# Two forward products of the second token block, in halves of 256 tokens, moved ahead of the first block's last two backward products

## The chip, the cores and the metric

The kernel runs on one core of a Trainium2 chip. The metric is the time of one execution in device microseconds; smaller is better. The core has five instruction streams that matter here, each of which runs its own list in order: TensorE (PE; its weight loads are shown as PEld), VectorE (DVE), ScalarE (ACT), GpSimd (POOL) and SyncE (SP), which here issues loads only. They meet through semaphores.

## The reference, cut to what matters

One call computes the output and all gradients of a mixture of two branches, for x of 2048 tokens by 1024 channels and a hidden width F of 3584:

```
g   = sigmoid((x * gate_w).sum(-1))          # one gate per token
a   = irfft2(rfft2(x) * (w_r + 1j * w_i))    # spectral branch
h   = x @ w1 + b1
out = g * a + (1 - g) * (relu(h) ** 2 @ w2 + b2)
```

and, for a given grad_out, the gradients of x, w_r, w_i, w1, b1, w2, b2 and gate_w. For the dense branch the backward pass needs db = (1 - g) * grad_out, then dh = 2 * relu(h) * (db @ w2.T), from which the gradients of w1, b1, w2 and x follow.

## The kernel before, in words

The kernel is one long program for TensorE with the other engines around it. It has an opening (up to about 80 us), in which x and grad_out are loaded, turned and first used; then the rest of the dense layer's forward and backward products, with the spectral branch's transforms dealt in between; then the gradients of w1 and w2, the gradient of x, and the output. Only the opening is touched by the change.

The tokens go in four blocks of 512 (`s` = 0 to 3), the hidden width in chunks of 128 rows; `fp` counts pairs of chunks and `c` the chunk in a pair. In the opening the first two pairs, so four chunks, go through all four blocks.

Per block of four tiles of 128 tokens, these steps follow one another:

- x is loaded by SyncE (`rows_of_x`, L1815), turned on TensorE into xT (`turn_x`, `turn_tile`, L709, through two PSUM buffers `pt`) and copied out of PSUM, mostly by ScalarE (L710).
- VectorE sums x * gate_w over the channels of each tile (`gate_of`, L724). `gate` (L727) makes 1 - g of the four sums on ScalarE (omg, L731, and gcol, L732) and multiplies the four tiles of grad_out by it on VectorE (L734).
- These four tiles (dbn) are turned on TensorE (`turn_grad`, L709) and copied to dbT, mostly by VectorE (L710).
- A forward product `forth(fp, s, c)` is eight matmuls of 128 x 512 (L820) into one PSUM bank (ph) and a ReLU on ScalarE (L821); after two of them ScalarE squares the pair (L795).
- A backward product `back_(fp, s, c)` is eight matmuls with w2T (L827) into a bank (pd), and one VectorE instruction (L831) that makes dh of it. Forward and backward products share two banks.

w2T is a part of w2 turned by the DMA while it is loaded. For these four chunks it is loaded in two halves, and the second half is read by the backward products of the second pair alone.

The first two forward products of the first block are already made in two parts of 256 tokens each: `half_hidden(c, h)` (L802) makes part `h` of chunk `c` with eight matmuls of 128 x 256 (L807). The first parts are issued as soon as two tiles of x are turned, and `hidden` (L813) adds the second part when the product's turn comes.

The order of all this is written out by hand: `mlp_in` is a generator that is advanced once per product, and the loop at L1865 takes a step of it between the turning of tiles, gates and loads. In the first round of that loop (`k` = 0) the steps are: three forward products; the turning of the first gradient tiles; the fourth forward product; the first backward product; x tiles 4 and 5 turned; the second backward product; x tiles 6 and 7 turned; the seventh step; stores, the gates of the second block, more loads of x, and the start of the spectral branch's first stage (`first_stage`, L743); the eighth step. The gradient tiles of the second block are turned in the next round.

`first_stage` adds and subtracts the halves of rows of x (`folds`, L270: L272, L273, L277, L278, L283 and L284 on VectorE, three small copies on ScalarE, L279 to L285), multiplies the result on TensorE (`row_stage`, L293; `column_stage`, L325). It reads x from tiles of its own (src), loaded by `ahead_to` (L736) on SyncE, two row tiles for one fold.

Within this order a scheduler of the framework places the instructions of each engine. `after(ins, earlier, NoSync)` (L250) ties an instruction in order behind another one without a semaphore; with the default it also waits. The first two instructions of a fold (L272 and L273), the gate sums L724 of all but the first block, and L293 are tied in this way to `later["last"]`, which is the newest L831 at the time when the line of the program is run. The third fold's loads (L741) wait for it.

Of the kernel before, what the change touches and what calls it, by code (L numbers as in the profile page):

```python
# [10 lines left out]
P = 128  # L11
# [130 lines left out]
def kernel(  # L142
# [107 lines left out]
    def after(ins, earlier, wait=mybir.DependencyClass.Sync):  # L250

        if earlier is not None:
            info = mybir.DependencyInfo(wait, mybir.DependencyReason.DATA)
            tc.add_manual_dep(ins.ins, earlier.ins.name, info, reason="paced")
# [440 lines left out]
    xT = xT_p.tile([P, DC, S], BF16, name="xT", tag="xT")  # L695
    dbT = xT_p.tile([P, DC, S], BF16, name="dbT", tag="dbT")

    later = {}
# [71 lines left out]
    def mlp_in():  # L770
# [5 lines left out]
        SW = 512  # L776
# [11 lines left out]
        def h_bank():  # L788
            return mps.tile([P, SW], FP32, name="ph", tag="ph", bufs=2)
# [9 lines left out]

        begun = {}  # L800

        def half_hidden(c, h):  # L802
            if h == 0:
                begun[c] = h_bank()
            part = slice(h * SW // 2, (h + 1) * SW // 2)
            for dc in range(DC):
                one = mm(  # L807
                    begun[c][:, part], lhsT=w1[0][:, dc, c * P : (c + 1) * P], rhs=xT[:, dc, part],
                    start=h + dc == 0, stop=dc == DC - 1, skip_group_check=True,
                )  # L810
            later.setdefault("halves", []).append(one)

        def hidden(fc, ss, w1g, rT):  # L813
            if fc in begun:
                half_hidden(fc, 1)
                ph = begun.pop(fc)
            else:
                ph = h_bank()
                for dc in range(DC):
                    later["newest"] = mm(ph[:], lhsT=w1g[:, dc, fc % 2 * P : (fc % 2 + 1) * P], rhs=xT[:, dc, ss], start=(dc == 0), stop=(dc == DC - 1))  # L820
            nc.scalar.activation(rT, ph[:], ACT.Relu, bias=b1col[:, fc : fc + 1])  # L821
# [14 lines left out]
        def load_w2(fg, earlier=None, halves=(0, FGW // 2)):  # L836

            if fg not in w2T:
                w2T[fg] = wb.tile([P, DC, FGW], BF16, name="w2T", tag="w2T", bufs=2)
            for h in halves:  # L840
                f0 = fg * FGW + h
                after(turned(w2T[fg][:, :, h : h + FGW // 2], B_w2[f0 : f0 + FGW // 2, :]), earlier)

        w1, h2, dh, rTs = {}, {}, {}, {}
# [3 lines left out]
        def load_w1(fp):  # L848
            w1[fp] = f1.tile([P, DC, PW], BF16, name="w1f", tag="w1f") if fp == 2 else wb.tile([P, DC, PW], BF16, name="w1g", tag="w1g", bufs=2)
            ld(out=w1[fp][:], in_=w1v[:, :, fp * PW : (fp + 1) * PW])  # L850
# [12 lines left out]
        def forth(fp, s, c, by_rows=False):  # L863
            first, at = (s % 2 == 0, s % 2) if by_rows else (c == 0, c)
            if first:
                pair[0] = new_rT()
            rT = pair[0][:, at, :]
            hidden(2 * fp + c, rows_(s), w1[fp], rT)
            rTs[fp, s, c] = rT
            if not first:  # L870
                out = h2_of(fp, s // 2)
                squared(pair[0][:], out[:, c] if by_rows else out[:, :, s % 2, :])
            if c == 1 and s % 2 == 1:
                store(h2T_scr, h2.pop((fp, s // 2)), fp, s // 2)
# [131 lines left out]
        load_w1(1)  # L1006
        yield
        half_hidden(0, 0), half_hidden(1, 0)
        load_w2(0, halves=(0,))
        yield  # L1010
        load_w2(0, halves=(FGW // 2,))
        yield
        waiting = []
        for s in range(4):
            for what in (forth, back_):
                for fp in range(2):
                    for c in range(2):
                        if s == 3 and what is back_:
                            waiting.append((fp, s, c))
                        else:  # L1020
                            what(fp, s, c)
                        if s == 2 and what is forth and fp + c == 0:
                            load_w2(1, later["last"])
                        yield
            if s == 1:
                load_w1(2)
        for _ in w_sums(2, True):
            pass
# [22 lines left out]
        for n, u in enumerate(units_):  # L1051
# [60 lines left out]
            waiting = [(u.fp, 2 * u.sp + j, c) for c, j in ((0, 0), (0, 1), (1, 1), (1, 0))]  # L1112
# [728 lines left out]
    warm(7)  # L1841

    units = mlp_in()
    rows_of_x(0, 2)
    vrow = f1.tile([FC + DC, P], BF16, name="vrow", tag="vrow")
# [143 lines left out]
```

## Time and profile before

| | |
|---|---|
| median of 3 runs | 1193.3 us (1192.56 to 1193.49) |
| the profiled execution's own time | 1191.93 us |
| its span, first to last instruction | 1190.2 us |
| TensorE busy | 1177.4 us, 7275 matmuls |
| VectorE / ScalarE / GpSimd busy | 895.3 / 531.5 / 387.6 us |
| DMA | 249.84 MB, mean 210 GB/s |

Lines of the profile give the start in us, the duration, the engine, the line of the program, the operation, what is written and read, and the count of like instructions in a row; in brackets stands the idle time of the engine just before, and what ended it. In the groups by line the columns are the busy time, the mean duration in ns, and the idle time before, with what ended most of it. Times are counted from the span's start.

### The profile page before, as it was taken

How to read it: one execution, taken by the hardware profiler on the slowest of the kernel's cores; microseconds unless marked ns; L12 is line 12 of the kernel's file. 1: busy time of each engine (PE TensorE's matmuls, PEld its weight loads, DVE VectorE, ACT ScalarE, POOL GpSimd, SP SyncE). 2: the span in 40 equal slices, each digit the busy share in tenths (PEclk: the TensorE clock that was granted, in tenths of full speed). 3: DMA queues.
4: the chain of work that ended last, by engine and by line, in shares of the span. 5: the costliest groups of instructions: out<-in, count | busy, mean ns of one | idle time of the engine just before them, and what ended most of it. 6: DMA issues, size and time to landing. Idle time of an engine off the chain costs nothing.

```text
span 1190.2 us, 19485 instructions
## 1 busy us (share of the span) xinstructions
PE 1177.4 (99%) x7275; PEld 640.5 (54%) x7275; DVE 895.3 (75%) x1598; ACT 531.5 (45%) x961; POOL 387.6 (33%) x618
## 2 busy tenths in 40 slices
PE   8999999999999999999999999999999999999998
PEld 5555555444444444444447999998544444444444
DVE  6888887788989887877637666676785777976757
ACT  5678888577777772444324666564100010000000
POOL 0234433555858573755231233221001110000000
PEclk9999999999999999999999999999999999999999
DMA  9997585677969779888997999995799999564530
GB/s 251 298 291 235 166 215 170 199 211 179 249 169 232 239 241 186 195 192 212 225 200 157 232 229 260 234 217 153 251 193 228 263 287 282 170 199 147 181 125 36
DMA packets 329464, 249.84 MB, mean 210 GB/s; under 512 B 187912, under 2 KB 287658, under 8 KB 328858
## 3 DMA queue, kind: packets, MB, share of 16 engines
q1 hardware_dynamic: 268352, 112.12, 44.2%
q0 software_dynamic: 35136, 111.72, 29.9%
q10 hardware_dynamic: 25882, 24.76, 7.0%
q8 instruction: 57, 0.93, 0.3%
q14 instruction: 37, 0.30, 0.1%
HBM read 114.82 MB, written 89.67 MB: 172 GB/s over the span
## 4 chain that ended last, share of the span: by engine, by line
PE 78%; DVE 14%; ACT 3%; issue 2%; DMA 2%; SPq 1%; ACTq 0%; DVEq 0%
PE pX L1275 15%; PE xX L1576 14%; PE pV L1275 12%; PE pd L827 11%; PE xV L1576 7%; PE ph L928 6%; PE xZ L1576 4%; PE ph L820 2%; PE pui L325 1%; DVE dhT L831 1%; DVE rT L947 1%; PE pki L635 1%; DVE tt L453 1%; PE pu L325 1%; PE pZ L928 1%
## 5 line engine op out<-in xcount | busy, mean ns | idle before, releaser
L827 PE MATMUL pd<-dbT,w2T 128*128 128x512 bf16 x896 | 210.1, 379 | 3.4 <-DMA w2T<-in_B_w_dram 1.5
L827 PEld LDWEIGHTS <-w2T 128*128 128x128 bf16 x896 | 86.4, 98 | 107.6 <-issue 6.2
L1576 PEld LDWEIGHTS <-dS 128*128 128x128 f16 x686 | 66.4, 98 | 79.0 <-issue 3.4
L831 DVE SCALAR_TENSOR_TENSOR dhT<-pd,rT 128x512 bf16<-128x512 f32 x112 | 76.6, 684 | 33.7 <-PE pd L827 32.9
L1627 POOL DMA_DIRECT2D out_dram<-ot x32 | 17.4, 544 | 246.1 <-DVE ot L1683 128.0
L1693 ACT ACTIVATE w2br<-w2br,dsc 128x512 f32<-128x512 bf16 x8 | 5.8, 724 | 174.5 <-DVE ot L1683 117.4
L1576 PE MATMUL xX<-oT,dS 128*128 128x512 f16 x336 | 76.4, 379 | 0.6 <-DVE eR L1605 0.5
L1291 ACT COPY u<-pX 128x512 f32<-128x512 f32 x56 | 32.8, 586 | 90.5 <-PE pX L1275 84.9
L1576 PEld LDWEIGHTS <-odd 128*128 128x128 bf16 (+1 forms) x462 | 44.8, 98 | 51.5 <-issue 0.9
L1576 PEld LDWEIGHTS <-even 128*128 128x128 bf16 (+1 forms) x448 | 43.6, 98 | 52.6 <-issue 0.7
L1275 PEld LDWEIGHTS <-T 128*128 128x128 f16 x672 | 64.6, 98 | 7.5 <-issue 0.2
L948 ACT ACTIVATE rT<-rT 128x512 bf16<-128x512 bf16 x69 | 43.4, 629 | 42.3 <-DVE rT L947 41.8
L795 ACT ACTIVATE h2T<-rT 128x1024 bf16<-128x1024 bf16 x56 | 59.6, 1065 | 0.2
L1295 DVE TENSOR_TENSOR whi<-pV,u 128x512 bf16<-128x512 f32 x28 | 19.3, 689 | 47.1 <-ACT u L1291 47.0
L491 POOL DMA_DIRECT2D y_scr<-pc x64 | 47.2, 738 | 22.7 <-DVE pc L488 12.9
L1275 PEld LDWEIGHTS <-S 128*128 128x128 f16 x336 | 32.5, 98 | 40.8 <-DVE S L1207 1.9
L453 DVE TENSOR_TENSOR tt<-x,w 128x1028 f16<-128x1028 f16 (+1 forms) x64 | 41.9, 689 | 11.0 <-issue 5.8
L1275 PEld LDWEIGHTS <-resL 128*128 128x128 bf16 x448 | 43.1, 98 | 4.9
L1275 PEld LDWEIGHTS <-resR 128*128 128x128 f16 (+1 forms) x448 | 42.9, 98 | 4.9 <-issue 0.2
L1295 DVE TENSOR_TENSOR wlo<-pV,u 128x512 bf16<-128x512 f32 x28 | 19.2, 687 | 32.0 <-PE pV L1275 31.9
L859 POOL DMA_DIRECT2D h2T_scr<-h2T x28 | 20.9, 746 | 67.1 <-ACT f L285 30.2
L239 POOL DMA_DIRECT2D r<-y_scr x48 | 28.0, 588 | 42.4 <-ACT re L614 33.1
(382 smaller groups left out, 2803.7 us busy)
## 6 DMA issues: line engine op xcount, KB each, us to landing
h2T_scr<-h2T POOLq DMA_DIRECT2D x28, 512.0 KB, 4.2
dhT_scr<-dhT POOLq DMA_DIRECT2D x28, 512.0 KB, 5.2
y_scr<-pc POOLq DMA_DIRECT2D x64, 128.0 KB, 4.2
ax_scr<-yo POOLq DMA_DIRECT2D x16, 512.0 KB, 5.3
out_dram<-ot POOLq DMA_DIRECT2D x31, 256.0 KB, 3.3
z<-z_scr ACTq DMA_DIRECT2D x60, 128.0 KB, 3.4
out_dram<-whi POOLq DMA_DIRECT2D x28, 256.0 KB, 5.2
out_dram<-wlo POOLq DMA_DIRECT2D x28, 256.0 KB, 4.8
```

The source lines that it names most:

```text
L239: st(out=a, in_=b) if stored else st(out=b, in_=a)
L453: V(out=tt[:, k, :, :, 0:W], in0=x[:, a : a + 2, :, 0:W], in1=by, op=ALU.mult)
L491: st(out=columns_of(y_scr, c, h), in_=pc[:, n])
L795: after(nc.scalar.activation(h2T, rT, ACT.Square), behind_, mybir.DependencyClass.NoSync)
L827: turn["PE"] = mm(pd[:], lhsT=w_[:, ec, fc % FGC * P : (fc % FGC + 1) * P], rhs=dbT[:, ec, ss], start=(ec == 0), stop=(ec == DC - 1),)
L831: return STT(out=dhT, in0=pd[:], scalar=2.0, in1=rT, op0=ALU.mult, op1=ALU.mult, accum_out=gb1part[:, fc, sb : sb + 1],)
L928: turn["PE"] = mm(acc[:], lhsT=lhs[:, t, :], rhs=rhs[:, t, :], start=start and t == 0, stop=t == KH - 1, skip_group_check=True,)
L948: nc.scalar.activation(rT, rT, ACT.Relu)
L1275: self.mm = mm(out, lhsT=lhs[:, t, m * P : (m + 1) * P], rhs=rhs[:, t, :], start=start and t + a == 0, stop=t == KH - 1, skip_group_check= ...
L1291: turn["ACT"] = nc.scalar.copy(out=t_[:], in_=self.X[:])
L1295: turn["DVE"] = self.added = V(out=self.half(row, j), in0=self.sums(acc), in1=self.sums(t_), op=ALU.add)
L1576: ins = mm(acc, lhsT=lhs[:, fc, :], rhs=rhs[:, fc, :], start=start and fc == 0, stop=fc == KH - 1 and bias is None, skip_group_check=True,)
```

## The change

The order of the products is put into a list, and in it the first two forward products of the second block (s = 1, pair 0, chunks 0 and 1) change places with the last two backward products of the first block (s = 0, pair 1, chunks 0 and 1). Before the first of the two is made, the first parts (256 tokens) of both are issued; each is completed by its second part when its turn comes. `half_hidden` gets the token block as an argument. No other line of the program is changed.

```diff
-        def half_hidden(c, h):
+        def half_hidden(c, h, s=0):
             if h == 0:
                 begun[c] = h_bank()
             part = slice(h * SW // 2, (h + 1) * SW // 2)
+            tokens = slice(s * SW + h * SW // 2, s * SW + (h + 1) * SW // 2)
             for dc in range(DC):
                 one = mm(
-                    begun[c][:, part], lhsT=w1[0][:, dc, c * P : (c + 1) * P], rhs=xT[:, dc, part],
+                    begun[c][:, part], lhsT=w1[0][:, dc, c * P : (c + 1) * P], rhs=xT[:, dc, tokens],
                     start=h + dc == 0, stop=dc == DC - 1, skip_group_check=True,
                 )
...
-                half_hidden(fc, 1)
+                half_hidden(fc, 1, ss.start // SW)
...
-        for s in range(4):
-            for what in (forth, back_):
-                for fp in range(2):
-                    for c in range(2):
-                        if s == 3 and what is back_:
-                            waiting.append((fp, s, c))
-                        else:
-                            what(fp, s, c)
-                        if s == 2 and what is forth and fp + c == 0:
-                            load_w2(1, later["last"])
-                        yield
-            if s == 1:
+        order = [(what, fp, s, c) for s in range(4) for what in (forth, back_) for fp in range(2) for c in range(2)]
+        order[6:10] = order[8:10] + order[6:8]
+        for n, (what, fp, s, c) in enumerate(order):
+            if s == 3 and what is back_:
+                waiting.append((fp, s, c))
+            else:
+                if n == 6:
+                    half_hidden(0, 0, s), half_hidden(1, 0, s)
+                what(fp, s, c)
+            if (what, fp, s, c) == (forth, 0, 2, 0):
+                load_w2(1, later["last"])
+            yield
+            if n == 15:
                 load_w1(2)
```

## The prediction

> **What bounds the kernel now.** I read the page first: busy shares, then the groups.
>
> ```profile
> PE 1177.4 (99%) x7275; PEld 640.5 (54%) x7275; DVE 895.3 (75%) x1598; ACT 531.5 (45%) x961; POOL 387.6 (33%) x618
> ...
> L827 PE MATMUL pd<-dbT,w2T 128*128 128x512 bf16 x896 | 210.1, 379 | 3.4 <-DMA w2T<-in_B_w_dram 1.5
> ```
>
> TensorE is busy for 1177.4 of 1190.2 us: what moves its instruction stream moves the end. The backward products (L827) lost 3.4 us to waits, of which 1.5 us is one wait for a load of w2T. The second half of that tile is first read by the third backward product, so this is the place that the diff touches. Next the timeline of TensorE there (start, duration, engine, line, operation, count, idle before):
>
> ```profile
> 23.71 1.06 PE L709 MATMUL pt<-identb,xsrc 128*128 128x128 bf16 x16
> 26.24 3.63 PE L827 MATMUL pd<-dbT,w2T 128*128 128x512 bf16 x16 [1.47 <-DMA w2T<-in_B_w_dram]
> 29.70 1.89 PE L820 MATMUL ph<-xT,w1g 128*128 128x512 bf16 x8
> 31.43 1.06 PE L709 MATMUL pt<-identb,dbn 128*128 128x128 bf16 x16
> ...
> 36.62 1.07 PE L293 MATMUL pk<-kf,f 128*128 128x128 f16 x16
> ...
> 40.80 1.90 PE L827 MATMUL pd<-dbT,w2T 128*128 128x512 bf16 x8 [0.20 <-DVE dbT L710]
> ```
>
> The last x transposes are issued by 24.61 (16 at 0.056), then TensorE waits until 26.24. After that it runs almost without gaps to 40.80, the first backward product of the second block. In the gaps' list of the whole run, all that wait after 41 us (3.6 us) wait for VectorE or ScalarE, none for a DMA: time lost or won before 41 us is not given back later.
>
> So VectorE has to be read in the same stretch, with ScalarE's gate and SyncE's loads:
>
> ```profile
> 25.38 1.22 DVE L724 SCALAR_TENSOR_TENSOR Sw<-xsrc,Sw 128x1024 bf16<-128x1024 bf16 x1
> ...
> 26.64 1.22 DVE L724 SCALAR_TENSOR_TENSOR Sw<-xsrc,Sw 128x1024 bf16<-128x1024 bf16 x1
> ...
> 28.86 1.67 DVE L734 TENSOR_SCALAR dbn<-dbn,omg 128x1024 bf16<-128x1024 bf16 x4
> 31.45 0.69 DVE L272 TENSOR_TENSOR uv<-src 128x1024 f16<-128x1024 bf16 x1 [0.92 <-DMA src<-in_A_x_dram]
> ```
>
> ```profile
> 27.91 0.21 ACT L731 ACTIVATE omg<-pgs 128x4 f32<-128x4 f32 x1 [1.62 <-DVE Sw L724]
> ```
>
> ```profile
> 23.29 3.75 SPq L741 DMA_DIRECT2D src<-in_A_x_dram x3
> ```
>
> The chain is: gate sums of tiles 6 and 7 (L724), the gate on ScalarE (L731), the four gradient tiles times the gate (L734), their transposes on TensorE at 31.43. The fold L272 stands behind all this in VectorE's list and yet waits 0.92 us: its rows of x (tile src) are there only at 31.45.
>
> **The change, part by part.** The changed kernel's instruction lists agree with those of before up to the x transposes at 23.71 and again from about 41 us on; SyncE has two loads moved (below), POOL nothing. Only 24.6 to 41 us has to be worked out.
>
> *TensorE.* Behind the x transposes now stand 32 products of 256 columns in place of 16 of 512 later. Rows: 16 of 256 in 1.75 (7.85 to 9.60), 8 of 512 in 1.73 (29.70 to 31.43); 32 x 0.109 - 16 x 0.216 = +0.04 us. They need no w2T. Their banks come free with the first two L831 (22.4 and 24.77 + 0.69 = 25.46; reached at 24.61 and 25.48), and their second parts need x tiles 6 and 7 (copied at 24.36 + 1.93 = 26.29; reached at 26.36). They fill 24.61 to 28.11; w2T came at 26.24. The wait of 1.47 us is gone. The third backward product also needs the bank of the first forward product: its last matmul is issued by 27.23, ReLU starts 0.2 later (as at 31.43, 31.63), takes 0.69, so 28.17. The product ends at 29.90. If nothing else had moved, 1.47 - 0.04 - 0.06 = 1.37 us would be won.
>
> *VectorE: the price.* The fold is tied in order behind the newest L831 at the time of writing the program. Before, that was the third; the third has moved behind, so now it is the second. The list now reads: second L831, L724 of tile 6, **L272**, L724 of tile 7, L273, L734 x4, L277, L278, third L831, L283, L284, the next fold's two, first copy of a gradient transpose, and so on. VectorE takes its instructions in order, so L272 now holds up the gate of tile 7 and all behind it. It is reached at 25.38 + 1.15 = 26.53 and its data come at 31.45. What is late is the load, not an engine: SyncE issued the second row tile only after w2T landed (the 3.75 us above holds 2.5 us of that wait), and every load ahead of it is the same in both kernels, so I take 31.45 again.
>
> From there, with the distances between starts in VectorE's rows (L272 0.61, L724 1.15, L273 0.61, L734 1.60 for four): L724 of tile 7 from 32.06 to 33.29; omg at 33.32 to 33.53 (ScalarE); L273 at 33.25; L734 at 33.86, the first gradient tile ready at 34.29. TensorE, done at 29.90, gets its next transposes at 34.34: **4.44 us idle** where there were 1.47. ScalarE waits at omg too, with the second ReLU behind it (33.6 to 34.3); the fourth backward product needs it but stands behind the transposes, so this costs nothing more.
>
> Then TensorE: 16 transposes to 35.24, seven matmuls of the fourth backward product to 36.76, then the row products (L293) that need the fold's result. VectorE: L734 ends 35.46, L277 and L278 36.67, third L831 37.29, L283 and L284 38.04 with their end; ScalarE's small copy (L285, 0.2) frees L293 at 38.31. Idle again: 1.55 us. L293 takes 0.89 (39.20), one matmul and two of the forward product of the second pair 0.65 (39.85). The third gradient tile's transposes need the copy of the first: VectorE does L272, L273 (37.96 to 39.17) and that copy by 39.85. Four hundredths, then 0.45 and six matmuls 1.30: 41.65. The fourth tile's transposes need the next copy: L277, L278, copy, 41.65. 42.15; four column products 0.29; the next forward product waits for ReLU of the one before (41.65 + 0.2 + 0.69 = 42.54), 1.73, and the other column products 0.23: 44.55. The copies of the last two gradient tiles end at 44.14, in time. So the backward product of 40.80 starts at 44.55.
>
> **Sum:** 44.55 - 40.80 = **+3.75 us**. SyncE's two moved loads (a later fold's rows, now ahead of two gradient tiles) I cost at nothing: 512 KB at the 386 GB/s of that stretch is 1.4 us, and those tiles, issued from 29.35 and landed 6.8 later, are scaled only at 49.40, 13 us on; uncovered it would be those 1.4. The instruction counts elsewhere are unchanged. The sum is a difference against the profiled execution (1191.93, span 1190.2); the median of the runs shown is 1193.3, 1.4 above it, and I add to the median: 1193.3 + 3.75 = 1197.0.
>
> The stretch is a chain behind one landing, so the sum follows that time one for one: break-even is 31.45 - 3.75 = 27.7. With the load there by 26.53, when L272 is reached, the end is 44.55 - 4.92 = 39.63, at best 1.2 us won: less than the 1.37 above, since the fold's own work still sits ahead of the gate.
>
> **Rivals.** *The cover holds (chance 0.13).* Not slower: the rows land before 27.7, VectorE hardly stops, and the filled wait is worth up to 1.2 us: 1192.1. For it: two loads are only 512 KB. Against it: the row with 0.92 us of wait at 31.45, and SyncE held until w2T lands at about 26.2; the issues then take 5.4 us to land.
>
> *The clock falls (0.15).* At the start of the run 16 transposes take 1.90 us, later 1.06:
>
> ```profile
> 4.14 1.90 PE L709 MATMUL pt<-identb,xsrc 128*128 128x128 bf16 x16
> ...
> 9.60 1.06 PE L709 MATMUL pt<-identb,xsrc 128*128 128x128 bf16 x16
> ```
>
> TensorE starts at about half speed. No row shows what an idle time of 4.4 us does; the longest one inside the run, 1.47, did nothing. If it starts again at half speed for as long as at the start (1.18 to some 6): transposes to 36.05, seven matmuls at 0.43 to 39.05, L293 to 40.76 instead of 39.20, so +1.5, giving 1198.6; if the slow time is over by 37.2, nothing, since TensorE waits for VectorE until 38.31 anyway. [...]
>
> *Part of it is hidden (0.05):* 1194 to 1195.5. *More stalls behind it (0.05):* if the loads also come later, each microsecond adds one: above 1199.
>
> **How the numbers follow.** The forecast, 1196 to 1198, has 0.62. The range 1195.5 to 1199.0 takes in forecast, clock and a little of the hidden case. About 0.2% (2.4 us) is what a measurement of this kernel can tell from no change; that is 1195.7, so slower 0.82, same 0.16, faster 0.02.
>
> **What would show it.** L272 waiting some 4.9 us for src in place of 0.92, on VectorE at 31.4; omg on ScalarE near 33.3; no wait of L827 for w2T; TensorE idle some 4.3 to 4.4 us ahead of the transposes of dbn, put down to L734, and 1.5 ahead of L293; the first backward product of the second block at about 44.5. Wrong if src lands before 28, or if the stall is there and the end does not move.

## The result, and the profile after

The changed kernel takes 1194.04 us (median of 22 executions, 1192.12 to 1200.27). The kernel before, run between them on the same chip, takes 1192.48 us (22 executions, 1189.98 to 1195.1). The ratio is 1.0021, with a 95% interval of 1.0011 to 1.0031: slower by 1.3 to 3.7 us. The direction is the forecast's. The size is not: 1194.04 lies below the range of 1195.5 to 1199.0.

The profiled execution of the changed kernel took 1195.43 us (span 1193.6), 3.5 more than that of before (1191.93, span 1190.2), nearly the 3.75 forecast for that pair. So one pair of profiles agrees with the forecast and the medians do not: that is the question of this study.

The page of the changed kernel (its line numbers are 1 or 2 higher from L807 on), busy shares and the group of the backward products:

```profile
PE 1174.1 (98%) x7198; PEld 643.2 (54%) x7291; DVE 895.3 (75%) x1598; ACT 531.0 (44%) x961; POOL 388.6 (33%) x618
...
L828 PE MATMUL pd<-dbT,w2T 128*128 128x512 bf16 x862 | 207.9, 380 | 3.7 <-DVE dhT L832 1.6
```

TensorE's work is what it was, within 0.3 per cent (some records are missing: 7198 products against 7291 weight loads). The wait for w2T is gone from the group's list. In its timeline (start, duration, engine, line, count; in brackets the idle time before and what ended it) the forecast stall is there:

```profile
23.93 1.06 PE L709 MATMUL pt<-identb,xsrc 128*128 128x128 bf16 x16
24.83 3.69 PE L808 MATMUL ph<-xT,w1g 128*128 128x256 bf16 x32
28.42 1.89 PE L828 MATMUL pd<-dbT,w2T 128*128 128x512 bf16 x7
34.16 1.89 PE L709 MATMUL pt<-identb,dbn 128*128 128x128 bf16 x16 [3.85 <-DVE dbn L734]
...
38.08 1.07 PE L293 MATMUL pk<-kf,f 128*128 128x128 f16 x16
...
44.27 1.89 PE L828 MATMUL pd<-dbT,w2T 128*128 128x512 bf16 x8
```

VectorE and ScalarE in the same stretch:

```profile
25.60 1.22 DVE L724 SCALAR_TENSOR_TENSOR Sw<-xsrc,Sw 128x1024 bf16<-128x1024 bf16 x1
...
31.26 0.69 DVE L272 TENSOR_TENSOR uv<-src 128x1024 f16<-128x1024 bf16 x1 [4.43 <-DMA src<-in_A_x_dram]
31.87 1.22 DVE L724 SCALAR_TENSOR_TENSOR Sw<-xsrc,Sw 128x1024 bf16<-128x1024 bf16 x1
...
33.62 1.67 DVE L734 TENSOR_SCALAR dbn<-dbn,omg 128x1024 bf16<-128x1024 bf16 x4
```

```profile
33.13 0.21 ACT L731 ACTIVATE omg<-pgs 128x4 f32<-128x4 f32 x1 [4.76 <-DVE Sw L724]
```

The fold L272 stands ahead of the last gate sum and waits 4.43 us for its rows (forecast 4.9); TensorE is idle for 3.85 us ahead of the transposes (forecast 4.3 to 4.4). The gate on ScalarE, the scaling of the gradient tiles and their transposes follow, as worked out: 33.13 (forecast 33.32), 33.62 (33.86), 34.16 (34.34), L293 at 38.08 (38.31), the second block's first backward product at 44.27 (44.55).

One line looks odd. The 16 transposes at 34.16 show 1.89 us where the same row showed 1.06: the granted clock had fallen. The table by stretches (columns: length; busy time of TensorE, its weight loads, VectorE, ScalarE and GpSimd with the count of instructions; then TensorE's granted clock, DMA share, GB/s):

```profile
30.30:33.71 3.41, 0.01 (x1) 0.00 (x0) 2.45 (x5) 0.58 (x3) 0.00 (x0) 1.00 1.05 383
33.71:37.13 3.42, 2.98 (x20) 2.15 (x21) 3.42 (x9) 1.61 (x4) 0.73 (x1) 0.50 1.05 388
```

A stretch of 3.41 us with nothing on TensorE is followed by one of 3.42 at half clock. It cost nothing here: L293 waits for VectorE and ScalarE until 38.08 in any case.

### The profile page after: what moved, and what is told of

Read it like the earlier page. It is cut to its first block, busy times and chain, and to the rows that moved or that the text cites. A ratio compares the mean times of both kernels' runs of the same rounds, so it can differ in the third digit from the quotient of the medians.

```text
span 1193.6 us, 19422 instructions
## 1 busy us (share of the span) xinstructions
PE 1174.1 (98%) x7198; PEld 643.2 (54%) x7291; DVE 895.3 (75%) x1598; ACT 531.0 (44%) x961; POOL 388.6 (33%) x618
## 4 chain that ended last, share of the span: by engine, by line
PE 72%; DVE 15%; issue 4%; DMA 3%; ACT 3%; POOL 1%; SPq 1%; ACTq 0%; another core or an unknown queue 0%; DVEq 0%; POOLq 0%
PE pX L1277 15%; PE xX L1578 14%; PE pV L1277 11%; PE pd L828 8%; PE xV L1578 7%; PE ph L929 4%; PE xZ L1578 3%; PE ph L821 2%; DVE rT L948 2%; DVE dhT L832 1%; PE pui L325 1%; DVE tt L453 1%; PE pki L635 1%; PE pu L325 1%; PE pk L293 1%
## 5 line engine op out<-in xcount | busy, mean ns | idle before, releaser
L832 DVE SCALAR_TENSOR_TENSOR dhT<-pd,rT 128x512 bf16<-128x512 f32 x112 | 76.5, 683 | 33.4 <-PE pd L828 33.0
```

Source lines behind the costliest of these rows:

```text
L832: return STT(out=dhT, in0=pd[:], scalar=2.0, in1=rT, op0=ALU.mult, op1=ALU.mult, accum_out=gb1part[:, fc, sb : sb + 1],)
```

## The experiments

**How they are read.** All happens between the last x transposes of the opening (L709 on xsrc, 16 in a row, at 23.71 before and 23.93 after) and the first backward product of the second block (40.80 and 44.27). I call that stretch the opening time: 17.09 us before, 20.34 after, in the two first profiles. It is the right quantity, since the span less the moment of that product is nearly fixed: 1149.3 to 1150.1 us in twelve of the fourteen profiles of this study (1151.1 and 1151.9 in the other two). What is lost ahead of it stays lost.

**Theory A:** the fold's place costs whatever its rows' landing costs, and that landing moves from execution to execution; the two first profiles happened to have it late. **Rival B:** the stall is paid in every execution, but something else gives 2 us back. **Rival C:** the difference is the granted clock, not the fold. By C, executions at full clock should be within 0.5 us of the kernel before.

### Further executions of both kernels

The changed kernel, unaltered, in a group of its own:

> The changed kernel once more, unaltered, for a second profile and more times. Theory A (a chain behind the landing of the fold's rows): in the profile of after, L272 starts at 31.26, when the rows land, and the first backward product of the second block 13.0 us later, at 44.27. Whatever the landing is in this execution, that distance stays 13.0 +- 0.3, and the execution's time moves with the landing, one for one; the executions of 1192 to 1194 us are those in which the rows land at 28 to 30. Theory B (the landing is much the same each time, and the loss is given back later in most executions): landing 31.0 to 31.5 here too, the opening ends near 44.3, and executions of 1193 us show fewer gaps after 45 us. Theory C (the clock): the slow executions are slow because TensorE runs at half speed after its idle time; an execution with clock 1.000 is within 0.5 us of before.

It took 1193.58 us (12 executions, 1192.01 to 1195.93) against 1191.73 for the kernel before (35): 1.0010, interval 0.9998 to 1.0022. Its profile, TensorE and then VectorE:

```profile
24.12 1.06 PE L709 MATMUL pt<-identb,xsrc 128*128 128x128 bf16 x16
...
31.96 1.07 PE L709 MATMUL pt<-identb,dbn 128*128 128x128 bf16 x16 [1.46 <-DVE dbn L734]
...
35.88 1.07 PE L293 MATMUL pk<-kf,f 128*128 128x128 f16 x16 [1.34 <-ACT f L285]
...
42.07 1.89 PE L828 MATMUL pd<-dbT,w2T 128*128 128x512 bf16 x8
```

```profile
29.06 0.69 DVE L272 TENSOR_TENSOR uv<-src 128x1024 f16<-128x1024 bf16 x1 [2.04 <-DMA src<-in_A_x_dram]
```

Same instructions, same order; only the rows come 2.2 us earlier (29.06, not 31.26). The stall ahead of the gradient transposes shrinks from 3.85 to 1.46, and 44.27 becomes 42.07. From L272 to the backward product it is 13.01 us in both.

The executions whose mean granted clock is 1.000 speak against C: in this group the seven of the changed kernel have a median of 1193.05 us, the 28 of the kernel before 1191.63.

Then two more profiles of the changed kernel and two of the kernel before:

> A further profile of the changed kernel. Theory A (a chain behind the landing of the fold's rows): from L272 to the first backward product of the second block 13.0 us, as in the two profiles so far (31.26 to 44.27, 29.06 to 42.07), wherever between 27 and 33 the rows land; TensorE's wait for L734 follows the landing.

> As after_look2: 13.0 us from L272 to the first backward product of the second block. If instead the landing is again near 29, the landing at 31.3 of the first profile was the rare case, and the forecast was made from it.

> A further profile of the kernel before. Theory A: L272 runs at 30.5 to 31.5, hardly waiting, since VectorE reaches it only then; an earlier landing saves at most the 0.9 us of its wait and the 1.5 us of w2T's. So the opening (x transposes of tile 6 to the first backward product of the second block, 17.1 us in the first profile) varies by less than 2 us here, and by as much as the landing does in the changed kernel (20.3 and 17.9 so far).

> As before_look1. Where an execution is above 1194, the profile shows a wait elsewhere than in this stretch.

They took 1193.16 and 1193.86 us (changed), 1190.37 and 1194.75 (before). The first profile of these two of the kernel before, TensorE and VectorE:

```profile
23.14 1.06 PE L709 MATMUL pt<-identb,xsrc 128*128 128x128 bf16 x16
24.03 3.62 PE L827 MATMUL pd<-dbT,w2T 128*128 128x512 bf16 x15
27.97 1.90 PE L820 MATMUL ph<-xT,w1g 128*128 128x512 bf16 x8 [0.32 <-DVE dhT L831]
...
38.76 1.69 PE L827 MATMUL pd<-dbT,w2T 128*128 128x512 bf16 x7 [0.20 <-DVE dbT L710]
```

```profile
29.42 0.68 DVE L272 TENSOR_TENSOR uv<-src 128x1024 f16<-128x1024 bf16 x1
```

No wait for w2T, none of L272 for its rows, and an opening of 15.62 us, not 17.09. The wait of 1.47 us that the moved products were to fill belongs to one execution of the kernel before, with late loads. All profiles of the two kernels, with those of their variants with a warm start (below):

| profile | own time, us | x transposes | L272 starts (us behind them) | its wait for rows | first backward product | opening, us |
|---|---|---|---|---|---|---|
| before, first | 1191.93 | 23.71 | 31.45 (7.74) | 0.92 | 40.80 | 17.09 |
| before, second | 1190.37 | 23.14 | 29.42 (6.28) | none | 38.76 | 15.62 |
| before, third | 1194.75 | 26.32 | 32.60 (6.28) | none | 41.94 | 15.62 |
| before, warm start | 1191.27 | 23.87 | 30.15 (6.28) | none | 39.49 | 15.62 |
| after, first | 1195.43 | 23.93 | 31.26 (7.33) | 4.43 | 44.27 | 20.34 |
| after, second | 1193.39 | 24.12 | 29.06 (4.94) | 2.04 | 42.07 | 17.95 |
| after, third | 1193.16 | 24.05 | 28.70 (4.65) | 1.75 | 41.71 | 17.66 |
| after, fourth | 1193.86 | 26.45 | 29.40 (2.95) | none | 42.41 | 15.96 |
| after, warm start | 1193.93 | 24.56 | 29.14 (4.58) | 1.69 | 42.15 | 17.59 |

Two constants come out of it. From L272's start to the backward product it is 9.34 to 9.35 us before and 13.01 after, in every row: 3.67 us more, of which the gate sum (1.15), the four scalings (1.60) and the third L832 (0.61), all now behind the fold, are 3.36. And VectorE reaches L272 by 6.28 us behind the x transposes before, but by 2.8 to 2.95 after. So the opening is the later of 6.28 and the landing, plus 9.35, in the one kernel, and the later of about 2.9 and the landing, plus 13.01, in the other. A landing at 4.6 to 4.9 is hidden in the first and paid in the second: +2.0 to +2.3. Only one at 6.28 or later is paid in both, and then the whole 3.67 shows. This is A. Against B: nothing that comes behind the backward product gives the time back.

Where the lateness comes from can be read in SyncE's rows. In all five profiles of the table in which L272 waits, it starts 5.2 to 5.3 us behind the issue of the second of its two loads: that is issued at 26.21 in the first profile of before and at 25.97, 23.78, 23.48 and 23.92 in those of after (first, second, third, warm start). So it is the issue that moves, not the transfer. Ahead of it SyncE's queue waits for w2T in the two first profiles, for 2.5 and 2.2 us; in six of the other seven it stands between the two issues for 1.0 us or less. Why w2T itself comes later in some executions stays open.

The third profile of before is the slowest of its four, yet its opening is the short one. From the opening on it is 3.2 us behind the second profile, by what happens at the start; a further 1.2 us is lost behind the opening. TensorE's rows there, and the table by stretches:

```profile
8.00 0.34 PE L719 MATMUL pgw<-vrow,identb 36*128 36x128 bf16 x3 [1.59 <-DMA vrow<-in_B_b_dram]
...
8.80 3.25 PE L807 MATMUL ph<-xT,w1g 128*128 128x256 bf16 x16
```

```profile
5.77:9.18 3.41, 1.82 (x19) 1.08 (x18) 0.88 (x2) 0.98 (x2) 0.00 (x0) 1.00 1.03 330
9.18:12.59 3.41, 3.41 (x23) 2.61 (x21) 1.24 (x2) 0.51 (x1) 0.00 (x0) 0.50 1.39 317
```

A late landing of vrow, then 3.41 us at half clock. The fourth profile of after has the same start (a wait of 1.89, then 16 products of 256 columns in 3.46 us, where 1.92 is usual) and is all about 2.4 us late. This spread is in both kernels, so it need not be part of the difference, but it is as large as the difference.

### The fold without its load

This kernel leaves out the spectral branch's share of two row tiles: the first fold works on gradient tiles that are there early.

```diff
-        f, kg = {0: folds(f1, xs[0], later["last"])}, {}
+        f, kg = {0: folds(f1, dbn[:, 0:2, :], later["last"])}, {}
```

> The changed kernel with the first fold working on the first two gradient tiles, which are in SBUF since 17 us, in place of its rows of x: so the spectral branch's share of these two row tiles is left out. All loads stay, and the order of the instructions on each engine stays. Theory A: L272 runs at 26.5 without a wait, TensorE does not wait for L734, the first backward product of the second block starts at 39.6 (40.80 in before), and the time is 1.2 us under before (0.9990), with a spread as narrow as that of before. If the loss lies in the halves of 256, in the shared banks or in anything else of the new order, it stays 1.5 to 2.5 us above before. Theory C agrees with A here, since the idle time goes as well.

It took 1192.3 us (12 executions, 1190.32 to 1199.54) against 1191.73: 1.0011, interval 0.9995 to 1.0028. VectorE and TensorE:

```profile
27.38 0.68 DVE L272 TENSOR_TENSOR uv<-dbn 128x1024 f16<-128x1024 bf16 x1
```

```profile
30.77 1.06 PE L709 MATMUL pt<-identb,dbn 128*128 128x128 bf16 x16
...
40.38 1.89 PE L828 MATMUL pd<-dbT,w2T 128*128 128x512 bf16 x8
```

With nothing to wait for, L272 starts at 27.38, the stall ahead of the transposes is gone, and 13.00 us later stands the backward product: an opening of 15.82 (from 24.56). The mechanism holds, but the gain of 1.2 us that I expected is not in the time. I had measured it against 17.09; against the usual 15.62 nothing is left to win. The median is also raised by slow executions: five of the twelve took more than 1195.5, all with a mean clock of 0.997 to 0.999; why so many here is not known.

### The fold behind the gate

```diff
-            nc.vector.tensor_scalar(out=dbn[:, i, :], in0=dbn[:, i, :], scalar1=omg[:, i : i + 1], scalar2=None, op0=ALU.mult)
+            later["scaled"] = nc.vector.tensor_scalar(out=dbn[:, i, :], in0=dbn[:, i, :], scalar1=omg[:, i : i + 1], scalar2=None, op0=ALU.mult)
...
-        f, kg = {0: folds(f1, xs[0], later["last"])}, {}
+        f, kg = {0: folds(f1, xs[0], later["scaled"])}, {}
```

> The changed kernel with the first fold tied in VectorE's order behind the four products L734 in place of the newest L831, as it stood in before. Theory A: no TensorE wait for L734; the gradient tiles are turned at 29.9. The fold still waits for its rows (31.3), and now the copy of the first gradient transpose stands behind it, so TensorE waits some 2.5 us for that copy near 32.5; the first backward product of the second block at 41.3, so 0.5 us above before and some 3 below the profile of after; median 1193.0 where before has 1192.5. If the order of the fold had no part in it, the time stays as that of the changed kernel.

It took 1191.5 us (12 executions, 1190.84 to 1194.45) against 1191.73: 0.9994, interval 0.9984 to 1.0004. VectorE and TensorE:

```profile
28.84 1.67 DVE L734 TENSOR_SCALAR dbn<-dbn,omg 128x1024 bf16<-128x1024 bf16 x4 [0.27 <-ACT omg L731]
30.43 0.69 DVE L272 TENSOR_TENSOR uv<-src 128x1024 f16<-128x1024 bf16 x1
```

```profile
40.44 1.89 PE L828 MATMUL pd<-dbT,w2T 128*128 128x512 bf16 x8
```

The order of the products is the changed one, the fold stands again behind the four scalings, and the loss is gone: the median is 2.1 us under the changed kernel's of the same group (1193.58), and the opening is 16.04 (from 24.40). I had expected 0.5 us more than before, from rows that land at 31.3; in this profile L272 does not wait. So the moved products by themselves cost about nothing and win nothing.

### The rows issued earlier

```diff
+        if k == 0:
+            ahead_to(0)
         if k + 1 < NT // 4:
             rows_of_grad(k + 1)
```

> The changed kernel with the first fold's two row tiles loaded ahead of the second block's four gradient tiles, which then land some 1.4 us later. The order on the other engines is that of the changed kernel. Theory A: the rows land near 27, L272 waits 0.5 us or so, the first backward product of the second block at 27.0 + 13.0 = 40.0, so 0.7 us under before (1191.8 where before has 1192.5), the clock at 1.000 throughout. If the gradient tiles, now later, take the place of the rows as the load that is waited for, L734 shows it and the gain is gone. Without theory A, no change from the changed kernel.

It took 1191.58 us (12 executions, 1190.1 to 1196.82) against 1191.73: 0.9996, interval 0.9982 to 1.001. The fold stays ahead of the gate, but its rows are there: the first L272 starts at 26.67 without a wait. What its profile lost elsewhere, TensorE and then VectorE:

```profile
36.65 0.61 PE L709 MATMUL pt<-identb,dbn 128*128 128x128 bf16 x8 [1.46 <-DVE dbT L710]
...
41.29 1.89 PE L828 MATMUL pd<-dbT,w2T 128*128 128x512 bf16 x8
...
71.50 0.61 PE L821 MATMUL ph<-xT,w1g 128*128 128x512 bf16 x2 [1.92 <-DVE dhT L832]
```

```profile
26.67 0.69 DVE L272 TENSOR_TENSOR uv<-src 128x1024 f16<-128x1024 bf16 x1
...
34.70 0.69 DVE L272 TENSOR_TENSOR uv<-src 128x1024 f16<-128x1024 bf16 x1 [1.52 <-DMA src<-in_A_x_dram]
...
70.75 0.69 DVE L832 SCALAR_TENSOR_TENSOR dhT<-pd,rT 128x512 bf16<-128x512 f32 x1 [2.48 <-DMA dhT_scr<-dhT]
```

In this execution the next fold's rows were the late ones (opening 17.44, from 23.85), and at 70.75 a store was. Still the median is that of before, within its interval (I had expected 0.7 below it), and 2.0 us under the changed kernel's 1193.58. This mends the loss without touching the order of VectorE.

### The fold early, the products as before

The kernel before, with only the fold moved to where the change put it:

```diff
+            later.setdefault("lasts", []).append(last)
...
-        f, kg = {0: folds(f1, xs[0], later["last"])}, {}
+        f, kg = {0: folds(f1, xs[0], later["lasts"][1])}, {}
```

> The kernel before with one edit: the first fold is tied behind the second L831 in place of the third, as it comes to stand in the changed kernel; the products keep their places. Opening means from here the time from the x transposes of tiles 6 and 7 to the first backward product of the second block: 17.09, 15.62 and 15.62 in the three profiles of before, 20.34, 17.95, 17.66 and 15.96 in the four of after. Theory A: the gate of tile 7 stands behind the fold's rows here too; with the rows 4.8 us behind the x transposes, as in the middle executions, the gradient tiles are turned some 7.8 us behind them, and the opening is about 17.7, so 2.1 us above before. If moving the products is what costs, and not the fold, the time is that of before.

It took 1195.18 us (6 executions, 1194.4 to 1199.17) against 1191.5 (23): 1.0040, interval 1.0027 to 1.0053. VectorE and TensorE:

```profile
29.00 0.69 DVE L272 TENSOR_TENSOR uv<-src 128x1024 f16<-128x1024 bf16 x1 [3.36 <-DMA src<-in_A_x_dram]
...
30.75 0.69 DVE L831 SCALAR_TENSOR_TENSOR dhT<-pd,rT 128x512 bf16<-128x512 f32 x1
```

```profile
31.51 3.58 PE L820 MATMUL ph<-xT,w1g 128*128 128x512 bf16 x8 [4.13 <-DVE dhT L831]
...
43.53 1.89 PE L827 MATMUL pd<-dbT,w2T 128*128 128x512 bf16 x8
```

It costs more than the whole change: 3.7 us in the medians, and an opening of 20.79 (from 22.74) where I expected 17.7. Of these 3.1 us, 1.5 is the landing, 6.26 us behind the x transposes in this profile where I had taken 4.8. For the rest I had overlooked a second thing behind the fold. The forward product needs the bank that the third L831 frees, so TensorE stops at once, 4.13 us. And there the clock falls with work to do: from 31.53 to 34.95 it is 0.50, and eight products take 3.58 us, not 1.89. So the moved products do win something, about 2 us of 3.7, but only against a stall that the same edit brings in.

### Late rows in the kernel before

Two tiles of the third block's gradient are loaded by SyncE ahead of the fold's rows:

```diff
-            rows_of_grad(k + 1)
+            rows_of_grad(k + 1, 2 if k == 1 else 4, 2 if k == 1 else 0)
...
+            rows_of_grad(2, 2)
             ahead_to(1)
```

> The kernel before with two gradient tiles of the third block (512 KB) loaded ahead of the first fold's rows, so that these land about 1.4 us later; the order on TensorE, VectorE and ScalarE is that of before. Theory A: the fold stands behind the gate, so a late landing costs little: L272 waits 0.5 to 1.0 us in place of 0, L734 does not wait, and the time is 0.3 to 0.8 us above before at most. In the changed kernel the opening followed the landing one for one over 2.6 us (31.26, 29.06 and 28.70, each 13.0 us ahead of the end of the opening), so it would have lost the 1.4 in full. If the landing bounds before as well, it loses 1.4 here too.

It took 1193.11 us (11 executions, 1191.69 to 1197.17) against 1191.5 (23): 1.0013, interval 1.0003 to 1.0024. VectorE and TensorE:

```profile
31.37 0.69 DVE L272 TENSOR_TENSOR uv<-src 128x1024 f16<-128x1024 bf16 x1 [1.64 <-DMA src<-in_A_x_dram]
```

```profile
40.73 1.69 PE L827 MATMUL pd<-dbT,w2T 128*128 128x512 bf16 x7 [0.20 <-DVE dbT L710]
```

The rows land 8.00 us behind the x transposes (23.37) and the product follows 9.36 later: an opening of 17.36. I had expected 0.3 to 0.8 us in the time and it is 1.6. The kernel before is bound by the same landing too, as soon as it is later than 6.28; it only starts to be so later. The same lateness in the changed kernel was not tried.

### A warm start

Six matmuls of zeros in place of two ahead of the wait for vrow, in the kernel before and in the changed one:

```diff
-    warm(2)
+    warm(6)
```

> The kernel before with four more products of zeros ahead of the first transposes of the bias rows, where TensorE waited 0.0, 0.40 and 1.59 us for their load in the three profiles. In the one with 1.59 the granted clock fell to one half for 3.4 us from 9 us on and all that follows came 3.2 us later than in the quickest. If the spread of before (1190.4 to 1195) comes from this: the clock stays at 1.000 in all executions, those above 1194 become rare or lose some 1.7 us, and the median moves by no more than 0.5 either way. If the spread has other sources, the executions above 1194 are as many as before, with the clock at 1.000.

> The changed kernel with six matmuls in place of two ahead of the wait for vrow at its start, so that TensorE's idle time and the fall of its clock there should not happen. The theory that the fold's place costs what the rows' landing costs expects an opening of 17.6 to 18.0 us in the usual execution against 15.6 of the kernel before, so a median 1.5 to 2.2 us above the kernel before (1.0013 to 1.0018), with the highest executions lower than without the six matmuls if they came from the start (below 1195.5), and still above 1196 if they came from rows that land late. The rival, that most of the difference between the two kernels is a matter of the clock at the start, expects the time of the kernel before with the same six matmuls, 1191.4, so a ratio of 1.000 or below.

The kernel before with them took 1191.37 us (11 executions, 1190.74 to 1191.89) against 1191.5: 0.9999, interval 0.9991 to 1.0008. The changed kernel took 1192.9 us (12 executions, 1192.21 to 1200.07) against 1192.19 for the kernel before as it is (17): 1.0007, interval 0.9991 to 1.0022. The changed kernel's profile, VectorE and TensorE:

```profile
29.14 0.69 DVE L272 TENSOR_TENSOR uv<-src 128x1024 f16<-128x1024 bf16 x1 [1.69 <-DMA src<-in_A_x_dram]
```

```profile
32.04 1.07 PE L709 MATMUL pt<-identb,dbn 128*128 128x128 bf16 x16 [1.10 <-DVE dbn L734]
...
42.15 1.89 PE L828 MATMUL pd<-dbT,w2T 128*128 128x512 bf16 x8
```

With no wait for vrow in either and a mean granted clock of 1.000 in both, the openings of the two profiles still differ by 1.97 us (17.59 and 15.62). That speaks against C, though the medians alone do not: they differ by 0.7 us where I had expected 1.5 to 2.2, and in this last group the interval holds both zero and +2.2 us. At a mean clock of 1.000 the medians of this group are 1192.75 (11 executions) and 1191.92 (14). None of the 11 executions of the kernel before with the warm start is above 1192 us, where six of 23 without it are; one of 1200.07 remains in the changed kernel.

No version here is faster than the kernel before by more than its interval.

## Why the prediction was wrong in size and right in sign

**The list of VectorE: right.** The tie to the newest L831 put the fold ahead of the last gate sum. Every time behind it came out within 0.3 us, in the one execution where the landing was late (31.26).

**"every load ahead of it is the same in both kernels, so I take 31.45 again": the step that failed.** The list of loads is the same; their landing is not a constant. The five profiles of the changed order in the table have L272 at 2.95 to 7.33 us behind the x transposes; 31.45 was the latest seen in either kernel without an edit to the loads, 7.74. I read one execution's wait as a property of the kernel. That the first pair of profiles came within 0.3 us of the forecast was luck: both executions had late rows. With a usual landing of 4.6 to 4.9 the same sum gives +2.0 to +2.3 in place of +3.75; the medians say +1.56 (1.3 to 3.7 by the ratio's interval). 1194.04 falls, by 0.04, into the case that I called partly hidden and gave 0.05, but I had no mechanism for it.

**"The wait of 1.47 us is gone": true of that execution, but it was neither usual nor binding.** The other three profiles of the kernel before that have no edit to the fold or the loads show no such wait. In the first profile the backward product came 9.35 us behind L272, as in all others; so the fold's landing set the end there, and the wait for w2T lay beside it. The two are not independent, though: the same late w2T held back the issue of the fold's second load.

**The point of no change, 27.7: wrong for the same reason.** It compared a changed kernel with early rows to a kernel before with late ones. Against the usual 15.62 the rows would have to land by 15.62 - 13.01 = 2.61 us behind the x transposes, and VectorE does not get to the fold by then. "At best 1.2 won" was therefore not there to win, as the fold without its load showed.

**The base.** I added to 1193.3, the median of three executions. With 22 it is 1192.48. That is 0.8 of the 3.0 us by which the forecast was too high; the size of the effect is the other 2.2.

**The clock: it fell, but its chance is not settled.** In the first profile it fell as the rival had it: the granted clock was 1.00 from 30.30 to 33.71, with TensorE idle, and 0.50 from 33.71 to 37.13, which is just ahead of the 37.2 up to which I had said it costs nothing; it cost nothing. In the early fold alone it was 0.50 behind an idle time of 4.13 us and lengthened eight products by 1.7 us (3.58 in place of 1.89). It also fell without a stall of that length: at the start of the third profile of before it was 0.50 behind a stretch in which TensorE was busy for 1.82 of 3.41 us. The chance of 0.15 was my estimate, and no run shows how often a stall of 4 us brings the clock down. The two profiles with one (3.85 and 4.13 us) both have it at 0.50; in the three with an idle time of 1.10 to 1.46 us ahead of the gradient transposes, those took 1.07 us as usual.

**The 1.55 us ahead of L293** are no gap in the first profile, as the slow transposes and products fill them; in the second they are 1.34.

**Still open:** executions above 1195.5 us. Of the changed kernel, with and without the warm start, 8 of 48 are that slow, and of the kernel before as it is 7 of 97 over all groups. In 14 of these 15 the mean granted clock is 0.996 to 0.999, but some quick executions show 0.999 too. A late landing at the opening, a clock that falls at the start, and a late store at 71 us are each seen in a profile and worth 1.5 to 3.5 us, but no profile was taken of an execution of 1198 or 1200.

## What to carry to other kernels

A profile is one execution. A wait on a DMA in it is a sample (here none to 4.43 us in the five profiles of the changed order), and a change that lives on such a wait, or that puts an instruction in front of one, has to be priced over several profiles: how far behind a fixed point of the same engine's work the data land, and when the waiting instruction is reached. An order tie to "the newest instruction so far" moves when the program around it is reordered; look at what it is tied to afterwards, and keep work that waits for a load behind the work that others wait for.

## What the runs showed of the hardware

The same loads in the same order on the same queue landed 4.58 to 7.33 us behind the same transposes in four executions of the changed order that waited for them, each time 5.2 to 5.3 us behind the issue of the second one; ahead of that issue the queue stood for 0.5 to 2.2 us, and the 2.2 is put down to w2T.

The granted clock was 0.50 from 33.71 to 37.13 in the first profile of after, where TensorE was idle for 3.85 us up to 34.16; 0.50 from 31.53 to 34.95 in the early fold alone, where it was idle for 4.13 us up to 31.51; and 0.50 from 9.18 to 12.59 in the third profile of before, where it had been busy for 1.82 of the 3.41 us ahead, with an idle time of 1.59. In the fourth profile of after, 16 products of 256 columns took 3.46 us behind an idle time of 1.89 us; in the rows-earlier execution they took 1.91 us behind one of 1.62 us, and at 71.50 there two products of 512 columns took 0.61 us (0.59 elsewhere) behind one of 1.92 us.
